# Attention decode with gradients on one core: four of the first ten loads are split into 112 rows and small transfers of the last 16 rows

## The chip, the core and the metric

The kernel runs on one core of a Trainium2 chip. The metric is the device time of one execution in microseconds (us); three executions of the kernel before gave 1275.3, 1276.09 and 1280.69, so its median is 1276.09 us. One further execution was profiled, and all durations below come from that one.

## The reference

There are 2 x 32 = 64 heads. Each has one query row, 8192 keys and 8192 values of 128 bf16 numbers. The output of the attention and the gradients of q, k and v are wanted:

```python
def _fwd_reference(q, k, v):
    scale = q.shape[-1] ** -0.5
    scores = jnp.einsum("bhqd,bhkd->bhqk", q, k) * scale
    p = _softmax(scores, axis=-1)
    return jnp.einsum("bhqk,bhkd->bhqd", p, v)

def reference(q, k, v, grad_out):
    _out, _vjp = jax.vjp(_f, q, k, v)
    _grads = _vjp(grad_out)
    return (_out, dq, dk, dv)
```

K and V are 64 x 2 MB each, and dK and dV, of the same size, are outer products of one row per head with the weights of its 8192 tokens. So 268 MB are read and 268 MB are written, with little arithmetic.

## The kernel before, in words

**Tiles.** The K or the V of one head is one tile of 128 partitions x 64 tokens x 128 numbers: 2 MB, 16 KB in each partition. Below, a *row* is the 16 KB of one partition. Ten such tiles stand in SBUF (`ring`, `RING = 10`). A tile is loaded, used, then overwritten in place by the gradient that belongs there (dV over K, dK over V; `outer`, L317), and stored from there.

**Order of the transfers.** Loads are issued by the SP queue through `load` (L121), in the order K of head 0, V of head 0, K of head 1, and so on; below they are load 1, load 2, load 3, ... Ten are asked for at the start, before any head is computed. Each later one goes into a place whose store has landed; `cleared` asks for it right after that store. Stores are issued by the ACT queue in `store` (L361), and ACT also does most of the copies of PSUM to SBUF (`ev`, L151). Six of the 128 stores go by the POOL queue in small pieces (`store_by_fifteen`), with tiny transfers (`turn`, L331) between them; after such a store a transfer of 32 bytes on SP (`between`, L114) goes ahead of the load. Store 1 and store 2 write the two tiles of head 0, store 3 and store 4 those of head 1.

**Order of the compute.** The loop over heads is written out by hand. In head h, eight steps j transpose the K tile (j = 0 to 3) and then the V tile (j = 4 to 7) on TensorE, ACT copies the transposed blocks out, and the products with q and with grad_out follow. In the same eight steps the previous head p = h - 1 is finished: its weighted sums, its outer products on VectorE, its first store after j = 3 and its second after j = 7. So store 1 is issued when head 1 has reached j = 3.

**Completion semaphores.** A transfer from SP or ACT tells that it has landed through a semaphore, which sixteen steps raise by 16. In the built program the SP and ACT transfers take eight such semaphores in turn, in the order in which the program was written down; below they are lanes 0 to 7. A transfer whose lane was used before waits, on its issuing queue, until the earlier transfer on that lane has landed. A queue issues in order, so what stands behind a waiting transfer waits too. The two small loads of q and grad_out (`nat`, L385, on ACT) come first in the order: they have lanes 0 and 2, and loads 1 to 6 have lanes 1, 3, 4, 5, 6 and 7. Store 1 comes next and has lane 0. Loads 7, 8 and 9 have lanes 1, 2 and 3, store 2 has lane 4, and load 10 has lane 5.

Of the kernel before, what the change touches and what calls it, by code (L numbers as in the profile page):

```python
# [23 lines left out]
RING = 10  # L24
AWAY = 10
LAST = 60


@with_exitstack
def kernel(  # L30
# [11 lines left out]
    nc = tc.nc  # L42
    B, H, Sq, D = q.shape
    Sk = k.shape[2]
    P = nc.NUM_PARTITIONS
# [35 lines left out]
    k_v = k.rearrange("b h (p n) d -> (b h) p n d", n=NT)  # L81
    v_v = v.rearrange("b h (p n) d -> (b h) p n d", n=NT)
# [30 lines left out]
    def between(out):  # L113
        nc.sync.dma_start(out=out, in_=q_rows[0:1, 0:16])  # L114

    todo = [(h, w) for h in range(BH) for w in range(2)]

    def load(place):
        h, w = todo.pop(0)
        heads[h].kv.append(place)  # L120
        nc.sync.dma_start(out=place[:], in_=(k_v, v_v)[w][h])  # L121

    def cleared(h, w):
        for a in away:
            a[0] -= 1
        if is_rare(h, w):
            away.append([AWAY, heads[h].kv[1 - w]])
        elif todo:
            load(heads[h].kv[1 - w])
        if todo and away and away[0][0] == 0:  # L130
            between(spare[0:1, 480:496])
            load(away.pop(0)[1])
# [225 lines left out]
    def store(h, w, a=0, b=NT, by=None):  # L358
        if is_rare(h, w):
            return store_by_fifteen(h, w)  # L360
        (by or nc.scalar).dma_start(  # L361
            out=(dv_v, dk_v)[w][h][:, a:b, :], in_=heads[h].kv[1 - w][:, a:b, :]
        )
# [25 lines left out]
    for i in range(2):  # L389
# [3 lines left out]
            out=qz[i][:, 0 : 4 * BH].rearrange("p (h z) -> p h z", z=4)[:, :, 3], in_=tps[:]  # L393
# [7 lines left out]
    with tc.manual_schedule():  # L401
        for place in ring:
            load(place)
        for h in range(BH):
# [5 lines left out]
            for j in range(NS):  # L410
# [35 lines left out]
                if x and j in (3, 7) and not (last and j == 7):  # L446

                    store(p, j // 7, by=nc.scalar if todo or p < LAST else nc.sync)
                    cleared(p, j // 7)
# [15 lines left out]
        h, x = BH - 1, heads[BH - 1]  # L465
# [64 lines left out]
```

## Time and profile before

| What | Value |
|---|---|
| median of three runs | 1276.09 us (1275.3 to 1280.69) |
| the profiled execution | 1275.3 us; its span, from the first to the last instruction, is 1273.5 us |
| busy share of the span | TensorE 85%, ScalarE 76%, VectorE 70%, GpSimd 8% |
| moved by DMA | 539.01 MB, on average 423 GB/s |
| busy time of the 16 DMA engines by queue | SP's q1 52.7%, ACT's q10 44.2%, POOL's q0 2.6%, instruction queues 0.5% and 0.1% |
| one row of 16 KB in a DMA engine | 0.611 us (the median of the 16 KB packets on q1 and on q10) |
| one completion packet of 4 bytes | 0.009 us |
| a load, from issue to landing (median) | 38.8 us for K, 38.6 us for V |
| a store from ACT, from issue to landing (median) | 19.3 us |

The profile is read as follows. The busy shares count an engine's own instructions; the DMA row of the sliced view counts how much of the time the 16 DMA engines moved packets. The time line of a queue shows when it issued each transfer. The trace has one landing event for each of the sixteen steps of a transfer's semaphore, so it shows when the first and the last of them came.

### The profile page before, as it was taken

The page shows a single profiled execution, that of the slowest core. Times are in us where ns is not written, and L with a number is a line of the kernel's source. Part 1 is how long each engine was busy: PE and PEld are TensorE (multiplying, and loading weights), DVE is VectorE, ACT ScalarE, POOL GpSimd, SP SyncE. Part 2 cuts the span into 40 slices and gives each one's busy share as a digit, 9 for nine tenths or more (in the row PEclk, how much of TensorE's full clock was granted, in tenths as well). Part 3 has the DMA queues.
Part 4 walks back from the last instruction along what each step waited for, and adds up shares of the span by engine and source line. Part 5 has one row for each costly group of instructions (what it writes and reads, how often), then busy time and mean ns, then how long its engine had stood idle before and what let it go on. Part 6 is the DMA issues. An engine that isn't in the chain of part 4 may idle for free.

```text
span 1273.5 us, 31594 instructions
## 1 busy us (share of the span) xinstructions
PE 1083.4 (85%) x13444; PEld 721.0 (57%) x13444; DVE 891.6 (70%) x1574; ACT 971.1 (76%) x1134; POOL 106.9 (8%) x194
## 2 busy tenths in 40 slices
PE   5999998769988869888888888888888888898895
PEld 4666665546655546555565555555555555565563
DVE  1888886658766658776667677677676776776685
ACT  5898886758877759777778777777786777787785
POOL 1001110001110000211000121000111000022000
PEclk9999998889998989899889998999898999898997
DMA  9999999999999999999999999999999999999997
GB/s 393 419 428 429 425 427 427 428 430 428 426 426 426 430 429 427 427 427 426 430 429 427 430 426 426 428 429 428 426 424 426 426 428 429 425 414 426 428 415 333
DMA packets 44552, 539.01 MB, mean 423 GB/s; under 512 B 10682, under 2 KB 10682, under 8 KB 10682
## 3 DMA queue, kind: packets, MB, share of 16 engines
q1 hardware_dynamic: 20026, 285.22, 52.7%
q10 hardware_dynamic: 16736, 239.15, 44.2%
q0 software_dynamic: 7648, 12.61, 2.6%
q8 instruction: 105, 1.72, 0.5%
q14 instruction: 37, 0.30, 0.1%
HBM read 268.47 MB, written 268.47 MB: 422 GB/s over the span
## 4 chain that ended last, share of the span: by engine, by line
DMA 75%; PE 16%; ACT 4%; DVE 3%; issue 1%; ACTq 0%; SPq 0%; DVEq 0%
DMA ring<-in_k_dram 51%; DMA ring<-in_v_dram 15%; PE tp L144 9%; DMA out_dram<-ring 7%; ACT ev L151 4%; PE raw L160 2%; PE acc L285 2%; DVE ring L317 2%; PE turned L177 2%; DMA spare<-in_q_dram 1%; DMA nat<-in_grad_out_dram 1%; DVE rawsb L171 1%; DVE ev L149 0%; PE misc L229 0%; ACT E_f L218 0%
## 5 line engine op out<-in xcount | busy, mean ns | idle before, releaser
L151 ACT CAST ev<-tp 128x1024 bf16<-128x1024 f32 x960 | 936.3, 1017 | 288.4 <-PE tp L144 237.8
L144 PE MATMUL tp<-ident_bf,ring 128*128 128x128 bf16 x8192 | 661.0, 226 | 151.0 <-DMA ring<-in_k_dram 67.4
L144 PEld LDWEIGHTS <-ring 128*128 128x128 bf16 x8192 | 516.2, 101 | 370.1 <-issue 239.8
L317 DVE TENSOR_TENSOR ring<-qd,dS 128x2048 bf16<-128x2048 bf16 (+1 forms) x256 | 305.4, 1214 | 0.3 <-PE acc L285 0.3
L317 DVE TENSOR_TENSOR ring<-qd,P 128x2048 bf16<-128x2048 bf16 x255 | 305.3, 1218 | 0.1
L171 DVE COPY rawsb<-raw 128x512 f32<-128x512 f32 x127 | 87.8, 692 | 236.2 <-PE raw L160 235.0
L285 PE MATMUL acc<-ring,wz 128*32 128x512 bf16 x2048 | 211.2, 404 | 1.4 <-DVE wz L232 1.4
L160 PE MATMUL raw<-ev,qz 128*4 128x512 bf16 x2048 | 205.1, 390 | 0.1
L341 POOL DMA_DIRECT2D out_dram<-ring x126 | 70.7, 562 | 959.8 <-DVE ring L317 610.8
L177 PE MATMUL turned<-ident_f,rawsb 128*128 128x128 f32 x512 | 90.7, 305 | 11.6 <-DVE rawsb L171 10.2
L149 DVE CAST ev<-tp 128x1024 bf16<-128x1024 f32 x64 | 78.4, 1225 | 16.3 <-PE tp L144 15.7
L160 PEld LDWEIGHTS <-qz 128*4 128x4 bf16 x2048 | 46.6, 81 | 56.4 <-issue 6.2
L177 PEld LDWEIGHTS turned<-ident_f,rawsb 128*128 128x128 f32 x512 | 60.6, 154 | 26.7 <-DVE rawsb L171 25.3
L285 PEld LDWEIGHTS <-wz 128*32 128x32 bf16 x2048 | 52.7, 93 | 30.6 <-issue 3.0
L229 PEld LDWEIGHTS misc<-ld,ones_f 128*128 128x128 f32 x256 | 38.6, 190 | 15.2 <-DVE ld L256 10.9
L229 PE MATMUL misc<-ld,ones_f 128*128 128x1 f32 x256 | 46.1, 249 | 0.4 <-DVE ld L256 0.4
L209 DVE TENSOR_REDUCE gm<-misc 1x1 f32<-1x128 f32 x64 | 17.8, 279 | 38.5 <-PE misc L207 38.5
L331 POOL DMA_DIRECT2D spare<-in_q_dram x56 | 33.0, 588 | 120.3 <-DMA out_dram<-ring 102.3
L203 DVE TENSOR_REDUCE mp<-turned 128x1 f32<-128x64 f32 x64 | 14.1, 220 | 25.1 <-PE turned L177 23.9
L215 DVE TENSOR_SCALAR negm<-misc 128x1 f32<-128x1 f32 x64 | 9.8, 153 | 24.1 <-PE misc L213 24.1
L213 PE MATMUL misc<-gm,ones_f 1*128 1x1 f32 x128 | 24.2, 256 | 0.0
L213 PEld LDWEIGHTS misc<-gm,ones_f 1*128 1x128 f32 x128 | 18.7, 183 | 6.8 <-issue 0.4
(46 smaller groups left out, 283.1 us busy)
## 6 DMA issues: line engine op xcount, KB each, us to landing
out_dram<-ring ACTq DMA_DIRECT2D x114, 2048.0 KB, 19.3
ring<-in_k_dram SPq DMA_DIRECT2D x64, 2048.0 KB, 38.8
ring<-in_v_dram SPq DMA_DIRECT2D x64, 2048.0 KB, 38.6
out_dram<-ring SPq DMA_DIRECT2D x5, 2048.0 KB, 20.3
out_dram<-ring SPq DMA_DIRECT2D x6, 1024.0 KB, 10.7
out_dram<-ring POOLq DMA_DIRECT2D x6, 704.0 KB, 15.2
out_dram<-ring POOLq DMA_DIRECT2D x48, 64.0 KB, 21.1
out_dram<-ring POOLq DMA_DIRECT2D x24, 128.0 KB, 22.3
```

What stands on the lines that cost most here:

```text
L144: nc.tensor.matmul(tp[:, i, :], lhsT=x.kv[w][:, n, :], rhs=ident_bf[:], start=True, stop=True)
L149: nc.vector.tensor_copy(out=ev[:], in_=tp[:])
L151: nc.scalar.copy(out=ev[:], in_=tp[:])
L160: nc.tensor.matmul(raw[32 * k : 32 * k + 4, :], lhsT=qz[w][:, at : at + 4], rhs=evs[k // 2][:, 4 * (k % 2) : 4 * (k % 2) + 4, :].rearrange ...
L171: copy(out=x.raw[:], in_=raw[:])
L177: nc.tensor.transpose(out[:, i], x.raw[:, i * P : (i + 1) * P], ident_f[:])
L213: nc.tensor.matmul(mb, lhsT=ones_f[0:1, :], rhs=x.gm[:], start=True, stop=True)
L229: nc.tensor.matmul(x.lsum, lhsT=ones_f[:], rhs=x.ld[:, w : w + 1], start=True, stop=True)
L285: nc.tensor.matmul(acc[32 * g : 32 * g + 32, :], lhsT=wz[w][:, n // 4, at : at + 32], rhs=rows[:, n : n + 4, :].rearrange("p n d -> p (n d)"),
L317: nc.vector.tensor_tensor(out=x.kv[1 - w][:, n : n + size, :].rearrange("p n (d t) -> p n d t", t=2), in0=row.unsqueeze(1).to_broadcast([P ...
L331: nc.gpsimd.dma_start(out=two(spare[0:n, :])[:, :, i : i + 2], in_=two(q_rows[0:n, :])[:, :, 0:2])
L341: nc.gpsimd.dma_start(out=dst[own], in_=src[own], max_dma_last_dim=size)
```

## The change

Loads 4, 5, 6 and 7 (V of head 1, K and V of head 2, K of head 3) are no longer one transfer of 128 rows. Each is a transfer of the first 112 rows, and behind it the last 16 rows in transfers of their own: four transfers of four rows (loads 4 and 6) or two of eight rows (loads 5 and 7), taken with a step of 4 or 2 partitions. All stand on SP in the place of the load. 16 transfers take the place of four; nothing else is changed, and the instructions of the four compute engines stand in the same order in both programs. Because a program hands out lanes in turn, the later transfers have other lanes than before.

```diff
+UNEVEN = {(1, 1): 4, (2, 0): 8, (2, 1): 4, (3, 0): 8}
...
+    def in_parts(engine, out, in_, n):
+        engine.dma_start(out=out[: P - 16], in_=in_[: P - 16])
+        step = 16 // n
+        for i in range(step):
+            own = slice(P - 16 + i, P, step)
+            engine.dma_start(out=out[own], in_=in_[own])
+
     todo = [(h, w) for h in range(BH) for w in range(2)]
 
     def load(place):
         h, w = todo.pop(0)
         heads[h].kv.append(place)
-        nc.sync.dma_start(out=place[:], in_=(k_v, v_v)[w][h])
+        src = (k_v, v_v)[w][h]
+        if (h, w) in UNEVEN:
+            in_parts(nc.sync, place, src, UNEVEN[h, w])
+        else:
+            nc.sync.dma_start(out=place[:], in_=src)
```

## Prediction

> **What bounds the kernel now.** I read the page's slices first, then the queues.
>
> ```profile
> DMA  9999999999999999999999999999999999999997
> ...
> q1 hardware_dynamic: 20026, 285.22, 52.7%
> q10 hardware_dynamic: 16736, 239.15, 44.2%
> ```
>
> All 16 DMA engines are busy in every slice but the last, and the shares of the queues add up to 100%. The view by stretches of time says it more exactly (the two last columns are the DMA share and GB/s):
>
> ```profile
> 2.20:40.00 37.80, 25.88 (x312) 18.18 (x313) 12.59 (x27) 25.31 (x29) 2.50 (x5) 1.00 1.00 420
> 40.00:1200.00 1160.00, 1001.96 (x12462) 666.88 (x12459) 827.31 (x1457) 892.49 (x1026) 102.92 (x181) 0.94 1.01 427
> 1200.00:1240.00 40.00, 37.59 (x472) 24.95 (x472) 30.30 (x53) 33.24 (x38) 0.00 (x0) 0.96 1.00 424
> 1240.00:1273.50 33.50, 17.94 (x205) 10.97 (x201) 20.34 (x35) 19.83 (x43) 0.00 (x0) 0.75 0.79 331
> ```
>
> From 2.2 to 1240 us no DMA engine rests. A head costs 2 loads and 2 stores, 8 rows each per engine: 32 x 0.611 = 19.6 us. Compute alone needs about 16.5 us for a head (stores 2 and 4 below: 45.91 to 62.37). So compute can make up lost time and the DMA engines cannot: **time in which DMA engines rest before 1240 us is added to the end.**
>
> Now the stage of the change, the time line of SP and of ACT's issues:
>
> ```profile
> 2.12 1.30 SPq L121 DMA_DIRECT2D ring<-in_v_dram  x1
> 3.46 0.53 SPq L121 DMA_DIRECT2D ring<-in_k_dram  x1
> 4.04 0.47 SPq L121 DMA_DIRECT2D ring<-in_v_dram  x1
> 9.17 0.33 SPq L121 DMA_DIRECT2D ring<-in_k_dram  x1
> 12.35 0.33 SPq L121 DMA_DIRECT2D ring<-in_v_dram  x1
> 14.18 0.33 SPq L121 DMA_DIRECT2D ring<-in_k_dram  x1
> 23.99 0.33 SPq L121 DMA_DIRECT2D ring<-in_v_dram  x1
> 53.06 0.33 SPq L121 DMA_DIRECT2D ring<-in_k_dram  x1
> ```
>
> ```profile
> 37.79 0.35 ACTq L361 DMA_DIRECT2D out_dram<-ring  x1
> 45.91 0.34 ACTq L361 DMA_DIRECT2D out_dram<-ring  x1
> 54.26 0.34 ACTq L361 DMA_DIRECT2D out_dram<-ring  x1
> 62.37 0.34 ACTq L361 DMA_DIRECT2D out_dram<-ring  x1
> ```
>
> The first fence shows loads 4 to 11. Load 7 goes at 9.17, when load 1 has landed on lane 1 (its last landing event is at 9.15); loads 8, 9 and 10 go when the grad_out load (12.33), load 2 (14.17) and load 4 (23.97) have landed. So **a lane's wait really holds SP**. All ten loads are out at 24 us, and they keep the engines busy until 66 us. Only load 11 waits for a store:
>
> ```profile
> SPq L121 <- DMA out_dram<-ring: 28.7, 1, 28.7
> ```
>
> **The change, part by part.**
>
> *Rows per engine.* By the change's own words the small transfers are for the first engines; I take one row for each. Then engines 0-3 get 11, 9, 11 and 9 rows of the four loads, 4-7 get 7, 9, 7 and 9, and 8-15 get 7 each. Against 32 that is +8, 0 and -4 rows: +4.9, 0 and -2.4 us at 0.611.
> [...] No view of before can show the numbers of engines.
>
> *More issues.* 12 more at 0.33 us are 4 us of SP, beside its wait of 28.7 us; their completion packets are 9 ns each. I cost both at nothing.
>
> *Lanes.* This is the dear part. Sixteen transfers in place of four shift who waits for whom. In the built program SP has, in this order:
>
> ```
> load 4: 112 rows lane 5, parts lanes 6, 7, 1, 2    (waits: -, -, -, load 1, grad_out load)
> load 5: 112 rows lane 3, parts lanes 4, 6          (load 2; load 3, part of load 4)
> load 6: 112 rows lane 7, parts lanes 0, 2, 3, 4    (part of load 4; STORE 1, part of 4, 112 of 5, part of 5)
> load 7: 112 rows lane 5, parts lanes 6, 0          (STORE 2; part of 5, part of 6)
> load 8: lane 1 (STORE 3); load 9: lane 2; load 10: lane 4 (parts of load 6)
> ```
>
> Before, no load up to the tenth waited for a store. Now load 6's first part waits for store 1, load 7 for store 2 and load 8 for store 3, with everything behind them on SP. The stores themselves come from compute: store 1 cannot go before 37.79.
>
> The walk, with 1.3 us from issue to first packet (load 1: 0.74 to 2.1) and 0.611 a row:
> - Load 3 ends at about 17.9 (between loads 2 and 4, which land at 14.17 and 23.97). From there engines 8-15 have 21 rows up to the end of load 6's 112, engines 4-7 have 23, engines 0-3 have 27: they run dry at 30.7, 32.0 and 34.4. The waits inside (load 6 for a part of load 4, about 24) come in time.
> - Store 1, issued at 37.79, starts at 39.1 and moves 8 rows until 44.0. Idle so far: 8.4, 7.1, 4.7 us. Its landing on resting engines is in no row of before (beside loads it took until 52.99). Bounds: load 1 took 8.4 us; a half store issued at 1254.78 first landed 3.7 us later, of which 8 x 0.309 moved data, so a whole one would need 6.1. I take 6.7: 44.5.
> - Load 6's parts go at 44.5 to 46 and keep engines 0-3 busy from 45.8. Store 2, issued at 45.91, starts at 47.2. Engines 8-15 and 4-7 rest 3.2 us, engines 0-3 1.8. Store 2 ends at 52.1 (53.1 on engines 0-3) and lands at 53.5.
> - Load 7 starts at 54.8: 2.7, 2.7 and 1.7 us more. Store 3 (issued 54.26) and load 7 then share the engines until 64 to 65; store 4 (62.37) bridges them until loads 8 to 13 come, issued together from 65.5 on. From there the engines are full again.
>
> Idle sums: 14.3 (8-15), 13.0 (4-7), 8.2 (0-3). With the rows given or taken: 14.3 - 2.4 = 11.9; 13.0; 8.2 + 4.9 = 13.1. **On each engine the loss is about 12.5 us**, and the moved rows are gone into it: after the rest all engines start level, so the intended unevenness is erased. One credit: before, at load 10, the last landing was 3.45 us behind the first and 2.1 behind the mean of the sixteen; that lag of the late engines is erased too. I take 1.5 off: **11 us**. Bounds: 9 (all stores at the low end, full 3.5 us credit) to 15 (8.4 us for each of three stores, no credit).
>
> *Compute.* In 13 to 62 us TensorE waits for no load in the profile. The parts of load 6 land near 49, and V of head 2 is first read at about 53: hidden. K of head 3 (load 7) lands at about 65.5 and is wanted at 62: head 3 starts some 4 us late, which compute (16.5 of 19.6 us) makes up.
>
> Sum: 1275.3 (the profiled execution: span 1273.5 and 1.8 around it) + 11 = 1286.3. The median of the runs is 0.8 above the profiled one: **1287 us**.
>
> **The rivals.**
> - *The unevenness helps (not slower).* Late in the run the engines are far apart: the load issued at 1168.86 landed first at 1184.52 and last at 1210.92, and the chain of waits starts its last 62 us, which are compute, at that last landing. Eight engines stand at the back, five in front (the 32-byte transfers, one packet each, always run near the front). If engines 8-15 are the back ones, 4 rows less bring that landing 2.4 us forward, or 4.9 where rows of loads alternate with rows of stores: 1271 to 1274. It decides if store 1's landing doesn't hold SP while the engines run dry, that is if it landed before about 29.5 us; it is issued at 37.79. It is also the case in which the lanes matter less than I read. 7 in 100.
> - *The rest is partly hidden.* In the last 33.5 us the DMA share is 0.79: 7 us of rest per engine. If a levelled start keeps the engines together to the end, the last landing moves forward and these 7 us take up a part: +4, 1280. Against it: the spread of landings grows step by step through the run (3.5 us at load 10, 6 at 200 us, 25 at 900), long after the change. 13 in 100.
> - *It is dearer.* The lanes of later stores cross too: store 8, on ACT, now waits for load 12 and store 9 for load 13, each two loads further on than compute needs. ACT copies for TensorE, so compute stands for perhaps 6 us each time; where the loads in flight run out, that is DMA rest as well: +17, 1293. Against it: four or more loads are out at that time. 12 in 100, the next sentences' case included.
>  [...]
> - *Forecast:* 68 in 100, own range 1284 to 1291.
>
> **How the numbers follow.** 0.5%, about what a measurement of this kernel tells from no change, is 6.4 us: same is 1269.7 to 1282.5. Of the first rival I give 3 to faster and 4 to same; the second is same but for 2; the forecast and the third are slower: faster 0.03, same 0.15, slower 0.82. The range leaves out the first rival, a part of the second and the far end of the third: 1280 to 1296.
>
> **What would show it.** Right: on SP, load 6's first part is issued at 44 to 46 us, load 7 at 53 to 55, load 8 at 64 to 67; the DMA share between 31 and 39 us is below 0.3; from 70 us on it is 1 again, and the spread of late landings is as before. Each store's issue up to the third is unmoved. Wrong: loads 8 to 10 out by 40 us with the DMA share at 1 (then the lanes don't bite); or the rest there with the end less than 6 us later (then the tail hid it, to be seen in the last stretch's DMA share); or ACT waiting for loads between 95 and 150 us with the DMA share below 1.

## The result, and the profile after

The changed kernel takes 1295.51 us (median of five runs, 1295.05 to 1296.0), the kernel before beside it 1275.3 us. The ratio is 1.0151, with a 95% interval of 1.0133 to 1.0169: 20.2 us slower by the medians. The profiled execution took 1295.33 us, its span is 1293.6 us, which is 20.1 us more than before. So the sign of the prediction holds, and so does its outer range of 1280 to 1296 us, by 0.5 us; the forecast's own range, 1284 to 1291, does not. Its 11 us were too small, and the traces show that most of the 20 us are not the rest of the DMA engines that it summed.

The page first, with the row of GB/s under the DMA row:

```profile
DMA  9999999999999999999999999999999999999997
GB/s 306 318 348 430 427 426 428 427 429 429 427 426 426 427 430 429 426 427 427 428 430 427 428 428 426 427 431 427 429 426 427 424 427 428 429 420 425 426 407 334
```

The same row of the page of before:

```profile
GB/s 393 419 428 429 425 427 427 428 430 428 426 426 426 430 429 427 427 427 426 430 429 427 430 426 426 428 429 428 426 424 426 426 428 429 425 414 426 428 415 333
```

The DMA row is the one of before, 9 in every slice. What changed stands under it: the first three slices (97 us) move 306, 318 and 348 GB/s, where those of before move 393, 419 and 428 and the later ones, up to the last two, 420 to 431. The DMA engines were occupied and moved less. The stretches of time of the kernel after say it more sharply (the last two columns are DMA share and GB/s):

```profile
2.20:31.00 28.80, 17.73 (x208) 12.98 (x209) 4.91 (x15) 18.18 (x22) 2.51 (x5) 1.00 1.00 325
31.00:39.00 8.00, 8.00 (x109) 5.04 (x110) 7.88 (x13) 7.29 (x8) 0.00 (x0) 1.00 0.99 205
39.00:47.00 8.00, 7.33 (x99) 5.10 (x97) 5.36 (x12) 6.99 (x10) 0.00 (x0) 1.00 0.99 318
47.00:55.00 8.00, 6.36 (x85) 3.83 (x82) 7.93 (x13) 6.32 (x7) 0.00 (x0) 1.00 0.93 388
55.00:67.00 12.00, 1.54 (x13) 0.94 (x14) 0.15 (x1) 0.44 (x1) 0.00 (x0) 0.59 0.97 318
67.00:80.00 13.00, 11.38 (x133) 8.28 (x129) 7.01 (x13) 9.56 (x12) 0.00 (x0) 0.86 0.93 271
80.00:95.00 15.00, 14.13 (x191) 9.07 (x188) 12.07 (x23) 13.16 (x17) 0.00 (x0) 1.00 1.01 429
```

and two of the same stretches of the kernel before:

```profile
31.00:39.00 8.00, 7.97 (x108) 4.75 (x108) 7.55 (x13) 7.28 (x9) 0.00 (x0) 1.00 1.00 424
...
67.00:80.00 13.00, 12.33 (x169) 8.19 (x166) 11.04 (x20) 11.35 (x15) 0.00 (x0) 1.00 1.02 431
```

Between 31 and 39 us the share is 0.99 after and 1.00 before, and the rate 205 against 424 GB/s: a row takes nearly twice as long. The packet records give the median 16 KB row of SP's queue in steps of 4 us: 0.611 us up to 16 us, 0.95 at 16 to 20, then 1.16, 1.17, 1.16, 1.23, 1.25 and 1.15 until 44 us; 0.85 to 1.26 again between 56 and 76 us; 0.61 from there on. These are the times at which the four split loads move: by the landing events the 112 rows of load 4 have landed by 28.4 us, those of load 6 by 51.7, and the last part of load 7 by 76.4. The rows of ACT's stores keep 0.611 us beside them at 44 to 60 us.

The waits on SP that the prediction built on are there too. The time line of SP after (L121 is a transfer of 112 rows, L125 its small parts, L136 a whole load):

```profile
2.13 1.21 SPq L121 DMA_DIRECT2D ring<-in_v_dram  x1
3.38 8.85 SPq L125 DMA_DIRECT2D ring<-in_v_dram  x4
14.11 0.34 SPq L121 DMA_DIRECT2D ring<-in_k_dram  x1
20.32 7.37 SPq L125 DMA_DIRECT2D ring<-in_k_dram  x2
28.42 0.32 SPq L121 DMA_DIRECT2D ring<-in_v_dram  x1
52.91 2.58 SPq L125 DMA_DIRECT2D ring<-in_v_dram  x4
58.32 0.32 SPq L121 DMA_DIRECT2D ring<-in_k_dram  x1
58.69 1.71 SPq L125 DMA_DIRECT2D ring<-in_k_dram  x2
67.66 0.35 SPq L136 DMA_DIRECT2D ring<-in_v_dram  x1
```

Load 6's first part stood behind store 1 until 52.91, load 7 went at 58.32, load 8 at 67.66. The longest wait on SP, and the one of TensorE for the value tile of head 2, whose parts came so late:

```profile
SPq L125 <- DMA out_dram<-ring: 24.1, 1, 24.1
```

```profile
PE tp L159 <- DMA ring<-in_v_dram: 12.1, 1, 12.1
```

Yet the engines had work during nearly all of SP's 24.1 us (28.8 to 52.9): the last parts of load 4, load 5 and the 112 rows of load 6 were in their queues, at nearly twice the time a row.

**The balance up to 80 us.** Per DMA engine, the table counts rows moved (bytes divided by 16 KB and by 16), the time that rows took above 0.611 us each (0.309 for half rows), and the time in which nothing moved. The column "short" is the rows missing against before, times 0.611 us; "slower" and "rest" are the differences to before. All of it is worked out from the packet records of the profiled executions; the last column is the measured medians. The other five kernels of the table are the experiments below.

| kernel | rows | time above 0.611 | rest | short, us | slower, us | rest, us | whole run, us |
|---|---|---|---|---|---|---|---|
| before | 125.3 | 2.0 | 1.6 | | | | |
| after | 92.2 | 20.1 | 3.5 | 20.2 | 18.1 | 2.0 | +20.2 |
| slow rows, no waits on stores | 93.4 | 21.5 | 1.3 | 19.5 | 19.5 | -0.3 | +18.6 |
| waits on stores, whole loads | 102.3 | 3.0 | 14.6 | 14.0 | 1.0 | 13.1 | +13.9 |
| split evenly, 64 and 64 rows | 125.7 | 1.7 | 1.5 | -0.3 | -0.3 | 0.0 | -0.5 |
| load 4 uneven | 119.3 | 5.3 | 1.5 | 3.6 | 3.3 | -0.1 | +4.5 |
| load 4 in the same pieces, meant to be shared out evenly | 119.4 | 5.4 | 1.6 | 3.6 | 3.4 | 0.0 | +4.3 |

Behind 80 us the kernels before and after are alike: 8.8 and 8.2 us of extra row time up to 1180 us, a DMA share of 0.79 in the last 34 to 36 us, and 27.3 and 26.8 us between the first and the last landing event of a load issued at 1081 or 1082 us. So the 20.2 us are lost before 80 us, 18.1 of them to slower rows and 2.0 to rest.

### The profile page after: what moved, and what is told of

Its sections match the earlier page's. It is cut to its first block, busy times and chain, and to the rows that moved or that the text cites. A ratio compares the mean times of both kernels' runs of the same rounds, so it can differ in the third digit from the quotient of the medians.

```text
span 1293.6 us, 31620 instructions
## 1 busy us (share of the span) xinstructions
PE 1081.7 (84%) x13444; PEld 718.3 (56%) x13444; DVE 890.8 (69%) x1574; ACT 972.3 (75%) x1134; POOL 107.1 (8%) x194
## 4 chain that ended last, share of the span: by engine, by line
DMA 72%; PE 15%; ACT 6%; issue 3%; DVE 3%; ACTq 0%; SPq 0%; DVEq 0%
DMA ring<-in_k_dram 54%; PE tp L159 8%; DMA ring<-in_v_dram 7%; DMA out_dram<-ring 5%; ACT ev L166 5%; DMA spare<-in_q_dram 3%; DVE ring L332 2%; PE raw L175 2%; PE acc L300 2%; PE turned L192 2%; DMA nat<-in_grad_out_dram 1%; DVE rawsb L186 1%; ACT E_f L233 0%; PE misc L244 0%; PE misc L318 0%
```

## The experiments

Two theories stood against each other. **W**: the engines lose time because SP waits for stores. **R**: the rows of the split loads are slow whatever SP does.

**Slow rows without the waits.** The small parts are issued by POOL, so that SP's transfers have the lanes of before and no load up to the tenth waits for a store:

```diff
         for i in range(step):
             own = slice(P - 16 + i, P, step)
-            engine.dma_start(out=out[own], in_=in_[own])
+            nc.gpsimd.dma_start(out=out[own], in_=in_[own])
```

> The four loads go as 112 rows on SP as in the changed kernel, but their last 16 rows go on the POOL queue, in the same small transfers. [...] Theory W (the prediction: waits for lanes cost the time, rows move at 0.611 us): at most 2 us over before, about 1277, ratio 1.000 to 1.002. Theory R (the rows of a 112-row load move slowly, 1.1 to 1.2 us each in the trace of the changed kernel, and that sets the cost): 28 rows x about 0.55 us = 15 us over before, about 1291, ratio 1.011 to 1.013, with the DMA share near 1 and a low GB/s in the first 50 us.

1294.38 us, ratio 1.0148 (1.0131 to 1.0165). The first slices of its page:

```profile
DMA  9999999999999999999999999999999999999998
GB/s 261 296 425 429 428 425 426 427 429 429 426 426 427 427 428 428 427 427 428 428 428 428 429 426 426 428 428 427 426 421 426 427 427 429 428 425 427 427 411 337
```

R holds, and the loss is larger than the 15 us that it foresaw: without any added rest it is 18.6 us, and no load up to the tenth waits for a store. The median row takes 0.95 to 1.3 us from 12 to 52 us, then 0.611. How the slow time divides between the 112 rows and their parts is not shown: no run of the computation has one without the other, and here the parts are on another queue.

**The waits without slow rows.** All loads are whole; only five are asked for at the start, load 6 waits for store 1 and load 7 for store 2, then two go per store until ten are out:

```diff
-        for place in ring:
+        for place in ring[:5]:
             load(place)
+        held.extend(ring[5:])
...
     def cleared(h, w):
+            if held and h > 0:
+                load(held.pop(0))
```

> All loads are whole 128-row loads, but only five are asked for at the start; load 6 goes behind store 1 and load 7 behind store 2, and from store 3 on two loads go behind each store until ten tiles are in use. This has the waits of the changed kernel (a load behind each of the first stores) without its row form. By the walk of the prediction the engines run dry at 17.9 + 16 x 0.611 = 27.7 us and start store 1 at 39.1: 11.4 us of rest, and 1.8 more before load 6; less 1.5. Theory W (rest of the DMA engines early is added to the end): 11 to 13 us over before, about 1287 to 1289. Theory M (early rest is made up later or in the tail): under 5 us over before.

1289.63 us, ratio 1.0112 (1.0095 to 1.0129), 13.9 us. Its page and its stretch from 20 to 36 us:

```profile
DMA  7799999999999999999999999999999999999998
GB/s 327 301 425 427 429 425 426 428 429 427 427 426 427 428 429 429 427 427 426 429 429 428 428 426 427 428 428 429 428 425 428 426 428 427 429 413 424 425 417 336
```

```profile
20.00:36.00 16.00, 14.92 (x193) 10.22 (x193) 7.86 (x19) 14.62 (x18) 0.00 (x0) 1.00 0.45 188
```

Here the DMA row itself falls to 7: GB/s are low because engines rest. 13.1 us of rest and 1.0 us of slower rows up to 80 us became 13.9 us at the end. So the prediction's principle, that early rest is added to the end, is right. The walk gave 13.2 us of rest for this kernel, near the 13.1 found, and 11 to 13 us of loss with a credit of 1.5 taken off; the credit does not show. This holds for a kernel in which the rows stay at 0.611 us, and it has no load behind store 3 alone, as the changed kernel has.

The two pages beside each other are the way to tell these costs apart: **in these runs a low rate with the DMA row at 9 was slow rows (261 and 296 GB/s; 19.5 us of slower rows by 80 us and no added rest), a low rate with the DMA row below 9 was rest (327 and 301 GB/s at 7; 13.1 us of rest and 1.0 of slower rows).** The page of after is of the first kind.

**What makes a row slow.** A kernel with nothing but transfers, three loads of each form after one another, each into a tile that a tiny VectorE instruction then touches:

> Not the computation of the reference: only transfers, three of each form, form after form (128 rows; 112 from partition 0; 112 from partition 16; 96; 64; 64 into every other partition; 128 and 112 rows from a source with 32 KB from row to row; the last 16 rows; the same in fours; in eights; 64 and 64; a store of 128 and of 112 rows; 128 rows again). Theory W: each form moves its rows at 0.611 us, so 128 rows take 4.9 us a load, 112 rows 4.3. Theory S (slowness by where the rows stand in SBUF): 112 rows take 7 x 1.17 = 8.2 us a load from either end and from either source; 64 rows into every other partition differ from 64 rows into partitions 0 to 63. Theory H (slowness on the side of the source in HBM): the two forms from the source with 32 KB steps differ from those with 16 KB, and the two forms of 64 rows, with one source, are alike. In both S and H it is open whether the store of 112 rows is slow too.

The time line shows that instruction for each load, with what it waited for in brackets. Whole loads, 112 rows from partition 0, 64 rows into partitions 0 to 63, and the same 64 rows into every other partition:

```profile
18.70 0.06 DVE L121 MEMSET ring<- 128x1 uint32 x1 [5.02 <-DMA ring<-in_k_dram]
...
32.10 0.06 DVE L121 MEMSET ring<- 128x1 uint32 x1 [7.67 <-DMA ring<-in_k_dram]
39.79 0.06 DVE L121 MEMSET ring<- 128x1 uint32 x1 [7.63 <-DMA ring<-in_k_dram]
...
98.65 0.06 DVE L121 MEMSET ring<- 128x1 uint32 x1 [5.06 <-DMA ring<-in_k_dram]
...
108.39 0.06 DVE L121 MEMSET ring<- 128x1 uint32 x1 [2.39 <-DMA ring<-in_k_dram]
```

128 rows land 5.1 us after the load before them, 112 rows 7.7: the smaller transfer is the slower one. The same 64 rows take 5.1 us into neighbouring partitions and 2.4 into every other one. A second kernel of this kind, with further forms:

> Not the computation of the reference: only transfers, three loads of each form: 128 rows; 120; 32 into every fourth partition; 32 into partitions 0 to 31; 48 into every other; 64 into every other and 64 into the rest; four times 8 rows with a step of four partitions; four times 8 rows in a row; 128 again. Theory S: forms whose rows are spread over all partitions move at about 0.61 us a row, forms of neighbouring partitions that are not the whole 128 at 1.0 to 1.3 us; 120 rows are open (8 rows for each of 15 engines, or fewer engines): 4.9 us a load if only full rows per engine matter, 8 us or more if not.

Its line for a load of 120 rows:

```profile
42.89 0.06 DVE L103 MEMSET ring<- 128x1 uint32 x1 [9.43 <-DMA ring<-in_k_dram]
```

| form of the transfer into SBUF | us from landing to landing | median row, us |
|---|---|---|
| 128 rows | 4.8 to 5.1 | 0.611 |
| 120 rows from partition 0 | 9.4 to 9.5 | 1.25 |
| 112 rows from partition 0 | 7.2 to 7.7 | 1.05 |
| 112 rows from partition 16 | 6.8 to 7.3 | 1.03 |
| 96 rows from partition 0 | 6.4 to 6.9 | 1.11 |
| 64 rows, partitions 0 to 63 | 5.0 to 5.1 | 1.28 |
| 64 rows, every other partition of 128 | 2.1 to 2.4 | 0.613 |
| 64 and 64 rows, partitions 0 to 63 and 64 to 127 | | 1.25 |
| 32 rows, partitions 0 to 31 | | 1.28 |
| 32 rows, every fourth partition of 128 | 1.0 to 1.1 | 0.611 |
| 48 rows, every other partition of 0 to 95 | 3.1 to 3.4 | 1.07 |
| 8 rows, four partitions apart | | 0.611 |
| 8 rows, neighbours | | 1.31 |

Where two forms follow each other a row of the first can run into the second; the medians are of the loads within a form. Taking the rows from a source with twice the step changes nothing (128 rows 0.614 us a row, 112 rows 1.04), and the rows of stores of 112 rows, once the slow loads before them have ended, have a median of 0.611. So in these forms the slowness is on the side where SBUF is written, and it goes by which partitions are written together: the forms spread evenly over all 128 partitions ran at 0.61 us a row, and so did 8 rows four partitions apart; the contiguous pieces short of 128 (1.03 to 1.31), and every other partition of 0 to 95 (1.07), did not. The parts of the change with four rows had a median of 0.611 us here, those with eight rows, two partitions apart, one of 1.2 (0.7 to 1.8).

**The split alone.** Loads 4 to 7 as even partitions on SP and odd ones on POOL, 64 and 64 rows, a form that the table puts at 0.613 us:

```diff
+    def in_parts(out, in_):
+        nc.sync.dma_start(out=out[0:P:2], in_=in_[0:P:2])
+        nc.gpsimd.dma_start(out=out[1:P:2], in_=in_[1:P:2])
```

> Loads 4 to 7 are split in two, the even partitions on SP and the odd ones on POOL, 64 rows each, so each engine gets four rows of each and none is favoured; lanes of SP and ACT as before. Theory S (the 112-row form is slow because of where its rows stand in SBUF, and every-other-partition forms are not): within 2 us of before, about 1276, though the loads are split. Theory P (splitting a load, or the POOL queue beside SP at the start, is what costs, also in the run with 112 rows and POOL): 10 us over before or more.

1275.28 us, ratio 1.0001 (0.9991 to 1.001). Splitting four loads, and a second queue, cost nothing in this form. So what costs in the change is the form of its pieces; by the transfer kernels the 112-row piece is slow by itself (1.05 us a row), and so is the part of eight rows (1.2).

**The unevenness alone, by pieces at full speed.** The author's plan was to take four rows a load from eight engines and to give them to the eight others, so that eight have 12 rows of the load and eight have 4: the even partitions on SP, the odd ones as eight transfers of 8 rows, four partitions apart, on POOL, with small transfers between them that are meant to leave all eight on the same eight engines. That they do so is the author's assumption; no run shows which engine moved a row. First for loads 6, 7 and 8, 12 rows by this plan:

```diff
+    def in_parts(out, in_):
+        nc.sync.dma_start(out=out[0:P:2], in_=in_[0:P:2])
+        turn(11)
+        for lo in range(0, P, 32):
+            for i in (1, 3):
+                own = slice(lo + i, lo + 32, 4)
+                nc.gpsimd.dma_start(out=out[own], in_=in_[own])
+                turn(8)
+        turn(5)
```

> [...] Theory L (the intention of the change: the engines that fall behind are the last eight, and taking rows off them brings the end forward): 3 to 7 us under before, 1268 to 1273. Theory N (nothing is gained by moving rows early): within 2 us of before. Theory O (the wrong engines are relieved, or the small transfers run slowly): 4 us over before or more.

1302.15 us, ratio 1.0204 (1.0189 to 1.0219). Theories L and N fail. The time is in the range of theory O, but for a cause that O does not name, so the run tells nothing of the unevenness: POOL issued its 24 pieces mostly 2 to 6 us apart, the last at 99 us, TensorE stood waiting for them, and the DMA engines ran dry behind it:

```profile
PE tp L162 <- DMA ring<-in_v_dram: 26.2, 1, 26.2
PE tp L162 <- DMA ring<-in_k_dram: 15.5, 1, 15.5
```

```profile
100.00:115.00 15.00, 1.49 (x13) 0.89 (x13) 0.00 (x0) 0.39 (x1) 1.17 (x2) 0.50 0.75 253
115.00:127.00 12.00, 11.54 (x133) 8.44 (x129) 7.12 (x14) 9.62 (x12) 0.00 (x0) 0.84 0.31 128
```

So the same for load 4 alone, where POOL has the time (its pieces are out at 21 us), and for loads 4 and 8, four and eight rows by the plan:

> [...] SP's lanes stay as before. Theory L (an early gift of rows to the engines in front is kept to the end, so the late landings move forward): 4 rows x 0.611 = 2.4 us less, about 1272.9, and the last landing of the load near 1169 us comes some 2 us earlier against its first. Theory N (the spread of the landings is made anew through the run, so an early gift is gone by the end): within 1.5 us of the kernel before, the late spread still 25 to 27 us.

> [...] Theory L: 8 x 0.611 = 4.9 us less, about 1270.4. Theory N: within 1.5 us of the kernel before. If the POOL parts of load 8 come late, TensorE waits for V of head 3 between 75 and 95 us; a wait of up to 6 us there can be made up by compute, a longer one that empties the DMA engines is added and would make this run inconclusive.

1280.21 us, ratio 1.0035 (1.0021 to 1.0049), and 1284.7 us, ratio 1.0068 (1.0055 to 1.008): 4.5 us a load, slower. Both theories fail, the gift of rows by its sign and "no difference" by its size. The kernel with loads 4 and 8 is not inconclusive by its own condition: its DMA engines stay full, with a share of 1.00 from 60 to 80 us and 1.01 from 80 to 100. With load 4 alone:

```profile
20.00:36.00 16.00, 14.92 (x195) 10.21 (x193) 7.96 (x19) 14.62 (x18) 1.88 (x4) 1.00 1.01 317
36.00:47.00 11.00, 10.33 (x141) 7.11 (x138) 8.87 (x15) 9.90 (x13) 0.00 (x0) 1.00 1.01 427
```

Again a share of 1 at a low rate: from 20 to 36 us half of SP's rows (median 1.03 us) and nine in ten of POOL's (median 0.92) took longer than 0.7 us, although both forms run at 0.61 alone. Two reasons were thought possible, the wrong side or the unevenness itself; so load 4 alone was taken again, against this first kind with the rows meant for the other eight engines:

```diff
-        turn(11)
+        turn(3)
...
-        turn(5)
+        turn(13)
```

> [...] Theory side (the first kind cost time because it gave rows to the engines that are behind at the end): the sign turns, and 2 x 2.4 us less than the 1280.2 of the first kind, about 1275.4 or below. Theory step (any unevenness puts the engines out of step, and the rows are then slow, whichever side has more): again 4 to 5 us more than before, about 1280, with a rate near 320 GB/s at a DMA share of 1 between 20 and 36 us.

1280.03 us, ratio 1.0032 (1.0022 to 1.0041). If the rows went as meant, the side doesn't matter: had the eight rows' difference between the sides been kept, the two kernels would be 4.9 us apart by the estimate of 8 x 0.611, and they are 0.2. That left the unevenness and the pieces, and the last kernel is meant to have the pieces without it: it leaves out the small transfers between them, so that by the author's assumption they fall on both sides in turn and each engine has 8 rows of the load.

```diff
                 nc.gpsimd.dma_start(out=out[own], in_=in_[own])
-                turn(8)
```

> [...] Theory step (it is the unevenness that puts engines out of step and makes rows slow): within 1.5 us of the kernel before, about 425 GB/s between 20 and 36 us. Theory pieces (small POOL transfers beside SP's loads make rows slow, however they are shared out): 3 us or more above it, a rate near 320 to 330 GB/s there.

1280.06 us, ratio 1.0032 (1.002 to 1.0044), and its stretch from 20 to 36 us:

```profile
20.00:36.00 16.00, 14.92 (x195) 10.22 (x193) 7.93 (x19) 14.62 (x18) 0.00 (x0) 1.00 1.00 348
```

The cost is there without the small transfers too: 3.4 us of slower rows by 80 us (the other 0.9 us are not located). The unevenness is worth nothing that these runs can tell: 1280.21, 1280.03 and 1280.06 us for one side, the other and, as meant, neither. The late landings are alike too: between 1079 and 1100 us the first and last landing event of a load are 25.3 to 26.4 us apart in all three.

But this doesn't clear the unevenness altogether. Which engine moved which row is in no record, so that the pieces fell as meant is not shown. And in all three kernels, the last one included, the sixteen landing events of a load soon come in two groups of eight: for load 9 the ninth event is 5.8, 5.2 and 5.9 us behind the eighth, where it is 0.3 us behind in the kernel before and 0.02 in the even split. A kernel with these pieces and the engines in step is not among the runs, so whether the pieces make rows slow by themselves, or by putting the engines out of step, stays open.

## Why the prediction was right or wrong

**Right: what bounds the kernel, and that lost DMA time is added to the end.** Every row of the balance says so: what the 16 engines had not moved by 80 us, times 0.611 us a row of one engine, is the loss of the whole run, within 1 us.

**Right: the lanes hold SP, in the predicted order.** Load 6's part behind store 1, load 7 behind store 2, load 8 behind store 3. The times were later than foretold (52.9, 58.3 and 67.7 for 44 to 46, 53 to 55 and 64 to 67), since store 1, issued at 36.58, landed at 47.2 to 52.9 among the slow rows of load 6 (42.4 to 51.7) and not, as the walk had it, on resting engines.

**Wrong: "and 0.611 a row", for the split loads.** This is the step that failed. The walk gave the rows of the 112-row transfers and of the parts the duration of rows of whole loads. By themselves the 112-row transfers took 1.05 us a row and the eight-row parts about 1.2; in the changed kernel SP's median row stood at 1.15 to 1.25 us while the split loads of the start moved. 28 rows per engine, a sixteenth of 4 x 112, come in the 112-row transfers; at 1.16 us, the commonest median above, they are 28 x 0.55 = 15.4 us over, which leaves 2.7 of the 18.1 for the parts and for whole loads among them; at the 1.05 us of the transfer kernel they are 12.3, which leaves 5.8. These are estimates from medians. No row of before shows such a form, so the duration was the unknown cost that should have been bounded from both sides, and the range got its upper end from lanes instead. **So it is luck that 1295.51 us lies inside 1280 to 1296**: 18.1 of the 20.2 us come from a term that the sum does not have, and 2.0 from the one that it puts at about 12.5.

**Wrong in consequence: the rest.** The engines were to run dry at 30.7 to 34.4 us, with a DMA share below 0.3 between 31 and 39. It was 0.99: the same 21 to 27 rows of the walk, with store 1 beside the last of them, lasted until 42.4 to 51.7 us, the landings of load 6's 112 rows. The prediction named a share of 1 there as the sign that the lanes don't bite; they did bite, but slow rows filled the gap. The two costs are not added: alone, the slow rows cost 18.6 us and waits like these 13.9, together 20.2. Of the predicted 14.3, 13.0 and 8.2 us of idle time 2.0 on the mean came about, so the credit of 1.5 us and the bounds of 9 to 15 that hung on the walk can't be checked in this kernel. That the parts go to engines 0 to 3 and 0 to 7, one row each, and so the 7 to 11 rows a load of the three groups, was the author's assumption, and no run shows it: what the trace of after shows is sixteen landing events for a transfer of 112 rows, four for a part of four rows and eight for a part of eight. In the kernel with whole loads and a load behind each of the first two stores, the loss at the end was 13.9 us for 13.1 of rest and 1.0 of slower rows: no credit is to be seen. From 67 to 80 us the share was 0.93, so it was not back at 1 from 70 us on, but it was from 80.

**Not contradicted: more issues cost nothing.** The even split has four transfers more, on POOL, and its ratio is 1.0001; the twelve more on SP are in no run apart from the slow rows and the waits. The 12 in 100 of the dearer case count in a cost that each further transfer has by itself. No run shows one: the median of the even split is 0.5 us below that of before, and in the kernel before the first landing events of loads 5, 6 and 7 come at 27.44, 32.33 and 37.23 us, 4.9 apart, the time of 8 rows at 0.611.

**Half right: compute.** Its lateness was foretold as hidden and was larger: TensorE waited 12.1 us for V of head 2, and store 4 went at 75.20 and not at 62.37. It cost no more than the 2.0 us of rest, since split loads kept the engines busy (0.97 from 55 to 67 us).

**The rivals.** That unevenness helps: no run shows it. In the kernels with load 4 in pieces, the same pieces gave the same time with rows meant for one side, for the other and for neither, and the late landings came 25 to 26 us apart in all three; the unevenness of the change itself was not run without its slow rows. That the rest is partly hidden: not so, the last stretch has a share of 0.79 as before. The dearer case named a time near the one measured (1293), but by the lanes of later stores. ACT did wait 7.9 us for a load between 80 and 160 us, with the DMA engines full in that time (shares of 1.00 to 1.01 from 80 to 150 us), so it is not the mechanism.

## What to carry to other kernels

Read the row of GB/s under the DMA row before you name a DMA loss: in these runs a full share at a low rate was slow rows, and only a falling share was waiting. When an edit changes the form of a transfer (its rows, its first partition, its step), take the duration of a row as unknown and measure that form by itself: here 112 rows took longer (7.2 to 7.7 us) than 128 (4.8 to 5.1). And count the completion semaphores that extra transfers use up, since whole loads behind early stores cost one kernel here 13.9 us with only 1.0 us of slower rows.

## What the runs showed of the hardware that was not expected

A load of 112 rows of 16 KB took 7.2 to 7.7 us and one of 120 rows 9.4 to 9.5, where 128 rows took 4.8 to 5.1. 64 rows took 5.1 us into partitions 0 to 63, as long as 128 rows, and 2.1 to 2.4 into every other partition of 128. The number of rows doesn't explain it: a sixteenth of 112 rows is 7, and 7 x 0.611 = 4.3 us would be the estimate from the row of a whole load. The trace of the kernel after has sixteen landing events for a transfer of 112 rows, but which rows went to which engine is in no record here, so why they are slow is left open. Rows of forms that are fast alone also became slow together: 64 even partitions on SP with 8-row pieces on POOL, about 1 us a row, where the same even partitions with the odd ones as one transfer on POOL stayed at 0.613. Why is open as well.
